# The sign pass of a float64-to-float32 conversion, moved from ScalarE to GpSimd

## The chip, the cores and the metric

One core of one Trainium2 chip. The metric is the device time of a run in microseconds (us). Every run quoted here is of the fast state, but for the two kernels without attention near the end (micro and micro2): they ran once each, so their state is unknown. Ratios with an interval are computed as the mean time of one kernel's fast runs over the mean time of the other's fast runs in the same rounds, so they are not quite the ratio of the medians that are quoted beside them.

## The reference, cut to what matters

A sketched linear attention is followed by a token-mixing block. What matters here is the mixing: two 1088 x 1088 token weight matrices that arrive as float64 and are needed as float32.

```python
def reference(**kw):
    attn_out = _attn_ref(q, k, v, S1, S2)            # (4, 4, 1088, 32)
    x = attn_out.transpose(0, 2, 1, 3).reshape(4, 1088, 128)
    theta = x @ w_theta
    zr, zi = x * np.cos(theta), x * np.sin(theta)
    y = np.einsum('ts,bsd->btd', w_tok_r, zr) + np.einsum('ts,bsd->btd', w_tok_i, zi)
    u = x + y
    return u + np.maximum(u @ w_ch, 0.0)
```

## The kernel before

The weights come as 34 pieces of 128 x 544 float64 values, seen as pairs of 32-bit words. For each piece three ScalarE passes and two VectorE instructions build the float32 bits: the scaled high word is shifted left by 3, and a "step" is added whose low 16 bits come from the low word and whose high 16 bits (a float16 with the bits that restore the sign) come from the high word.

```python
    def load_f32(dst, src):
        ...
        st = stg.tile([P, PIECE], I64, tag="st", name="st")[:p, :n]        # 4 buffers
        nc.sync.dma_start(st, src)
        lo, hi = split(st)
        step = stg.tile([P, PIECE, 2], I16, tag="step", name="step", bufs=2)[:p, :n]
        x = dst.bitcast(I32)
        A.activation(dst, hi.bitcast(F32), AF.Copy, scale=2.0**-112)                            # L122
        A.activation(step[:, :, 1].bitcast(F16), hi.bitcast(F32), AF.Copy, scale=2.0**-60)      # L123, the sign pass
        A.activation(step[:, :, 0], lo.bitcast(U32), AF.Copy, scale=2.0**-29)                   # L124
        ts(x, x, 3, ALU.logical_shift_left)                                                     # VectorE, L85
        tt(V, x, x, step.rearrange("p n t -> p (n t)").bitcast(I32), ALU.add)                   # VectorE, L81
    # ... cut ...
    for i in range(NK):
        for n in range(0, S, PIECE):
            load_f32(wT[:, i, n:n + PIECE], w_tok[i][:, n:n + PIECE])
    with tc.high_priority(offset=p1 - p0 + 1000):     # batch 0's keys and queries, interleaved with the pieces
        keys([0], first=True)
        for g in range(NG):
            queries(0, g)
```

`A` is ScalarE, `V` and `ts` are VectorE. A scheduler fixes the order of instructions on each engine when the kernel is built.

Of the kernel before, what the change touches and what calls it, by code (L numbers as in the profile page):

```python
# [21 lines left out]
F32 = mybir.dt.float32  # L22
F16 = mybir.dt.float16
# [4 lines left out]
AF = mybir.ActivationFunctionType  # L28
ALU = mybir.AluOpType
# [14 lines left out]
def kernel(  # L44
# [11 lines left out]
    nc = tc.nc  # L56
# [21 lines left out]
    V, A = nc.vector, nc.scalar  # L78

    def tt(eng, o, a, b, op):  # L80
        eng.tensor_tensor(out=o, in0=a, in1=b, op=op)  # L81

    def ts(o, a, s1, op0, s2=None, op1=None):
        kw = {} if op1 is None else {"op1": op1}
        V.tensor_scalar(out=o, in0=a, scalar1=s1, scalar2=s2, op0=op0, **kw)  # L85
# [8 lines left out]
    def split(t):  # L94
        w = t.bitcast(I32).rearrange("p (n t) -> p n t", t=2)
        return w[:, :, 0], w[:, :, 1]
# [9 lines left out]
    def load_f32(dst, src):  # L106






        p, n = dst.shape
        if src.dtype == F32:
            nc.sync.dma_start(dst, src)
            return
        st = stg.tile([P, PIECE], I64, tag="st", name="st")[:p, :n]
        nc.sync.dma_start(st, src)
        lo, hi = split(st)
        step = stg.tile([P, PIECE, 2], I16, tag="step", name="step", bufs=2)[:p, :n]  # L120
        x = dst.bitcast(I32)
        A.activation(dst, hi.bitcast(F32), AF.Copy, scale=2.0**-112)  # L122
        A.activation(step[:, :, 1].bitcast(F16), hi.bitcast(F32), AF.Copy, scale=2.0**-60)  # L123
        A.activation(step[:, :, 0], lo.bitcast(U32), AF.Copy, scale=2.0**-29)  # L124
        ts(x, x, 3, ALU.logical_shift_left)
        tt(V, x, x, step.rearrange("p n t -> p (n t)").bitcast(I32), ALU.add)
# [502 lines left out]


    load_f32(w2.rearrange("p t n -> p (t n)"), w_sq.rearrange("p t n -> p (t n)"))
    A.mul(w2[:, 0], w2[:, 0], 1.0 / (2.0 * math.pi))
    def keys(bs, first=False):
# [10 lines left out]
# [3 lines that stand above are left out]
# [60 lines left out]
```

## Time and profile before

| | before |
|---|---|
| time, median of 4 runs | 401.69 us (400.59 to 402.77) |
| busy in the load stage, 10 to 92 us: ScalarE / VectorE / GpSimd | 74.8 / 69.6 / 0 us |
| batch 0's feature work begins on VectorE | 91.76 us |

The profile has one row for each engine: PE is TensorE's matmuls, PEld its weight loads, DVE VectorE, ACT ScalarE, POOL GpSimd. "Busy" counts instructions that run. An instruction that has been issued but is held up inside the engine counts as busy too. The lines themselves are shown in the prediction.

### The profile page before, as it was taken

To read this page: it belongs to the slowest core of one execution; us is meant where nothing else is said; L and a number is where in the kernel's file an instruction comes from. 1 tells how busy PE (TensorE), PEld (TensorE's weight loads), DVE (VectorE), ACT (ScalarE), POOL (GpSimd) and SP (SyncE) were. 2 spreads that over 40 slices of the span, in tenths; PEclk is the share of its full clock that TensorE was granted. 3 is DMA by queue.
4 is the path that set the end of the run, shared out by engine and by line. 5 is a ranking of instruction groups with operands and counts; after the bars stand their busy time and mean duration, and the time that the engine had idled before them with its cause. 6 is when DMAs were issued, how large, how long until landed. Compare 5 with 4: busy or idle time off the path is not lost.

```text
span 400.2 us, 4502 instructions
## 1 busy us (share of the span) xinstructions
PE 292.0 (73%) x1633; PEld 212.7 (53%) x1633; DVE 241.2 (60%) x618; ACT 148.3 (37%) x309; POOL 0.7 (0%) x6
## 2 busy tenths in 40 slices
PE   1720741261389999999453489999889999899995
PEld 0610540140367876878232366756567666667663
DVE  5788978888924457467676822376923459543111
ACT  3779999993043332210022022313032431132100
POOL 0000000000000000000000000000000000000000
PEclk9975575556569999999756558999959999989999
DMA  7677888830000121110000000120000100001100
GB/s 271 227 259 250 300 248 286 299 140 2 0 0 2 52 69 59 59 61 2 1 0 0 2 0 0 41 75 0 2 0 0 58 0 2 0 0 41 36 21 16
DMA packets 11606, 28.82 MB, mean 72 GB/s; under 512 B 1216, under 2 KB 5568, under 8 KB 11584
## 3 DMA queue, kind: packets, MB, share of 16 engines
q1 hardware_dynamic: 11584, 28.53, 21.5%
q8 instruction: 13, 0.21, 0.2%
q14 instruction: 9, 0.07, 0.1%
HBM read 26.30 MB, written 2.23 MB: 71 GB/s over the span
## 4 chain that ended last, share of the span: by engine, by line
PE 56%; DVE 20%; ACT 15%; DMA 6%; issue 1%; SPq 1%; DVEq 0%; ACTq 0%
PE y L604 28%; PE w L557 4%; DMA st<-w_tok 4%; ACT step L123 4%; ACT step L124 4%; PE w L577 3%; PE acc L341 3%; PE acc L436 3%; PE w L426 3%; DVE lv L81 3%; ACT wT L122 2%; DVE qp L81 2%; PE w L551 2%; PE w L618 2%; PE w L572 2%; DVE fl L88 2%
## 5 line engine op out<-in xcount | busy, mean ns | idle before, releaser
L604 PE MATMUL y<-wT,zst 128*128 128x384 f32 (+1 forms) x384 | 135.3, 485 | 0.4 <-DVE zst L81 0.4
L604 PEld LDWEIGHTS y<-wT,zst 128*128 128x128 f32 x384 | 69.1, 195 | 29.3 <-issue 1.3
L341 PE MATMUL acc<-ksl 128*128 128x128 f16 (+1 forms) x216 | 23.8, 273 | 17.8 <-DVE ksl L88 17.8
L555 ACT COPY qpT<-w 128x256 f32<-128x256 f32 x36 | 13.1, 369 | 51.7 <-PE w L551 51.5
L557 PEld LDWEIGHTS w<-kvbd,qpT 128*128 128x128 f32 x144 | 24.5, 239 | 13.7 <-ACT qpT L555 11.8
L341 PEld LDWEIGHTS <-ksl 128*128 128x128 f16 x216 | 18.2, 110 | 22.2 <-DVE ksl L88 11.5
L557 PE MATMUL w<-kvbd,qpT 128*128 128x64 f32 x144 | 26.7, 328 | 4.1 <-ACT qpT L555 3.8
L81 DVE CUSTOM_DVE_ANT_0 wT<-wT,step 128x1088 uint16<-128x1088 uint16 x34 | 24.3, 719 | 8.0 <-ACT step L124 7.8
L123 ACT ACTIVATE step<-st 128x544 f16<-128x544 f32 (+1 forms) x35 | 27.8, 794 | 0.0
L124 ACT ACTIVATE step<-st 128x544 int16<-128x544 uint32 (+1 forms) x35 | 27.3, 781 | 0.0
L574 ACT COPY xT<-w 128x384 f32<-128x384 f32 x12 | 5.8, 479 | 56.1 <-PE w L572 56.1
L85 DVE TENSOR_SCALAR tn<-w 128x384 f32<-128x384 f32 x12 | 6.7, 558 | 32.8 <-PE w L577 32.8
L551 PE MATMUL w<-ident,qp 128*128 128x128 f32 x72 | 15.8, 336 | 14.6 <-DVE qp L81 14.6
L122 ACT ACTIVATE wT<-st 128x544 f32<-128x544 f32 x34 | 22.9, 679 | 4.8 <-DMA st<-w_tok 4.8
L485 ACT COPY lv<-w 128x288 f32<-128x288 f32 x36 | 13.2, 401 | 22.0 <-PE w L484 21.9
L625 ACT ACTIVATE ot<-w 128x384 f32<-128x384 f32 (+2 forms) x16 | 6.1, 406 | 39.2 <-PE w L618 29.9
L551 PEld LDWEIGHTS w<-ident,qp 128*128 128x128 f32 x72 | 11.3, 190 | 15.9 <-issue 15.8
L81 DVE TENSOR_TENSOR ot<-ot,w 128x384 f32<-128x384 f32 (+2 forms) x16 | 6.9, 449 | 18.6 <-ACT ot L625 18.6
L436 PEld LDWEIGHTS acc<-ld_v,kp 128*128 128x128 f32 x144 | 17.0, 192 | 0.7
L436 PE MATMUL acc<-ld_v,kp 128*128 128x64 f32 x144 | 17.4, 274 | 0.0
L81 DVE TENSOR_TENSOR uT<-xT,y 128x384 f32<-128x384 f32 (+1 forms) x12 | 6.3, 527 | 17.0 <-PE y L604 17.0
L577 PEld LDWEIGHTS w<-w,xT 128*128 128x128 f32 x72 | 12.3, 247 | 7.0 <-ACT xT L574 6.4
(217 smaller groups left out, 502.2 us busy)
## 6 DMA issues: line engine op xcount, KB each, us to landing
st<-w_tok SPq DMA_DIRECT2D x34, 544.0 KB, 4.8
ld_k<-k_l SPq DMA_DIRECT2D x4, 576.0 KB, 3.9
ld_q<-q_l SPq DMA_DIRECT2D x4, 576.0 KB, 4.9
ld_v<-v_l SPq DMA_DIRECT2D x4, 576.0 KB, 6.0
out<-ot SPq DMA_DIRECT2D x8, 192.0 KB, 2.1
out<-ot SPq DMA_DIRECT2D x4, 128.0 KB, 1.8
st<-w_sq SPq DMA_DIRECT2D x1, 256.0 KB, 3.8
out<-ot SPq DMA_DIRECT2D x4, 32.0 KB, 1.8
```

The costliest lines, as they stand in the source:

```text
L81: eng.tensor_tensor(out=o, in0=a, in1=b, op=op)
L122: A.activation(dst, hi.bitcast(F32), AF.Copy, scale=2.0**-112)
L123: A.activation(step[:, :, 1].bitcast(F16), hi.bitcast(F32), AF.Copy, scale=2.0**-60)
L124: A.activation(step[:, :, 0], lo.bitcast(U32), AF.Copy, scale=2.0**-29)
L341: nc.tensor.matmul(gp[:, r0 * P:(r0 + s1 - s0) * P], ks[:, a, cs], ks[:, s0:s1, cs], skip_group_check=True, **kw)
L436: nc.tensor.matmul(kv[:, n], kp[:, i * H + 2 * n:i * H + 2 * n + 2].rearrange("p h i j -> p (h i j)"), vn[:, c, 2 * n:2 * n + 2].rearrange ...
L485: A.copy(lv[:, :, :, c].rearrange("p l t n -> p (l t) n"), lp.rearrange("p (x n) -> p x n", n=HR))
L551: nc.tensor.transpose(tr[:, n * P:(n + 1) * P], qp[:, i * H + 2 * n:i * H + 2 * n + 2].rearrange("p h i j -> p (h i j)"), ident)
L555: A.copy(qpT.rearrange("p n t -> p (n t)"), tr[:, :2 * P])
L557: nc.tensor.matmul(num[:, i * P + n * 2 * D:i * P + (n + 1) * 2 * D], qpT[:, n], kvbd[b][:, n], start=True, stop=True)
L577: nc.tensor.matmul(th[:, i * P:(i + 1) * P], xT[:, i * P:(i + 1) * P], w2[:, 0], start=True, stop=True)
L604: nc.tensor.matmul(yp[:, :t1 - t0], z, wT[:, i, t0:t1], start=(i == 0), stop=(i == NK - 1))
```

## The change

The intent is to take one of three passes from the engine that sets the pace and give it to an engine that does nothing.

```diff
         A.activation(dst, hi.bitcast(F32), AF.Copy, scale=2.0**-112)
-        A.activation(step[:, :, 1].bitcast(F16), hi.bitcast(F32), AF.Copy, scale=2.0**-60)
+        nc.gpsimd.tensor_scalar(out=step[:, :, 1].bitcast(F16), in0=hi.bitcast(F32), scalar1=2.0**-60,
+                                scalar2=None, op0=ALU.mult)
         A.activation(step[:, :, 0], lo.bitcast(U32), AF.Copy, scale=2.0**-29)
```

With the change the line numbers in the file are one higher from here on: ScalarE's third pass becomes L125.

## The prediction

> **What bounds the kernel now.** I read the busy shares by slice first, then the stretches, the waits, and last the chain of work that ended last. In the page of the kernel before, each slice is 10 us:
>
> ```profile
> PE   1720741261389999999453489999889999899995
> DVE  5788978888924457467676822376923459543111
> ACT  3779999993043332210022022313032431132100
> DMA  7677888830000121110000000120000100001100
> ```
>
> There are two parts. Up to about 92 us the token weights are loaded and converted (34 pieces of 128x544 float64), while batch 0's key and query work runs between the pieces. From about 111 us TensorE is nearly always busy. Between them lie 20 us of VectorE work alone. The change touches the first part only. Its stretches (columns: PE, PEld, DVE, ACT, POOL busy, granted clock, DMA share, GB/s):
>
> ```profile
> 10.00:92.00 82.00, 32.60 (x209) 25.52 (x209) 69.55 (x242) 74.76 (x129) 0.00 (x0) 0.65 0.73 245
> 60.00:70.00 10.00, 1.01 (x7) 0.48 (x7) 8.90 (x32) 10.00 (x17) 0.00 (x0) 0.50 0.83 285
> 92.00:112.00 20.00, 6.13 (x25) 4.55 (x26) 18.90 (x33) 2.37 (x6) 0.00 (x0) 0.52 0.01 1
> ```
>
> ScalarE is the fullest engine, 74.8 of 82 us, and has no gap at all from 60 to 70 us; VectorE is close behind with 69.6 us. So ScalarE sets the pace, but VectorE has only 12.5 us to spare. The groups of a piece, as they are in that stretch or on the page:
>
> ```profile
> L123 ACT ACTIVATE step<-st 128x544 f16<-128x544 f32 (+1 forms) x35 | 27.8, 794 | 0.0
> L124 ACT ACTIVATE step<-st 128x544 int16<-128x544 uint32 (+1 forms) x35 | 27.3, 781 | 0.0
> L122 ACT ACTIVATE wT<-st 128x544 f32<-128x544 f32 x34 | 22.9, 679 | 4.8 <-DMA st<-w_tok 4.8
> L81 DVE CUSTOM_DVE_ANT_0 wT<-wT,step 128x1088 uint16<-128x1088 uint16 x34 | 24.3, 719 | 8.0 <-ACT step L124 7.8
> L85 DVE TENSOR_SCALAR wT<-wT 128x544 int32<-128x544 int32 x34 | 14.4, 432 | 0.1
> ```
>
> VectorE's add waits for ScalarE's second step pass for 7.8 us in all; ScalarE in turn waits 4.8 us for the load. The chain shows where this reaches the end. Here are three consecutive pieces on it, and the point at which the conversion lets go (start, us, what):
>
> ```profile
> 66.34 0.71 ACT step L123
> 67.05 0.65 ACT step L124
> 67.70 0.54 ACT wT L122
> ...
> 90.30 0.72 ACT step L124
> 91.04 0.72 DVE wT L81
> 91.76 0.98 DVE fl L88
> ```
>
> One piece advances in 0.71 + 0.65 + 0.54 = 1.90 us. Batch 0's feature work on VectorE (the line fl) stands behind the last converted piece in VectorE's fixed order, and everything after follows from it. So a shift of this moment should move the end by nearly as much.
>
> **What the Trainium skill says.** First, "SBUF — State Buffer", section Who interferes with whom: GpSimd's only SBUF read and write ports are VectorE's second pair. A VectorE instruction in a 2-port mode contends for it, and one with two SBUF inputs contends with a GpSimd instruction that reads SBUF; whichever starts first holds the pair for its whole duration. The trace before has no GpSimd work beside VectorE, so it neither confirms nor denies this. Second, "VectorE: DVE Perf Modes", section The perf-mode tier table: a float32 tensor_scalar between SBUF tensors runs at 2x with both ports. The trace fits: the 544-element shift takes 0.432 us, while the 576-element two-input product on the same engine takes 0.75 us. So the shift, the add (two inputs), and most of the feature work are all contending instructions. Third, "GPSIMD Engine Reference", section Performance versus the Vector engine: a tight one-input loop took 1.8 cycles an element at 1.2 GHz, 769 ns for 512 elements. An estimate from it for 544 elements is 0.82 us. The only comparable instruction in the trace is a 128x128 select of 0.29 us on GpSimd; estimated by elements alone this would be 1.23 us for 544, an upper figure, as part of it is fixed. I take 0.8 us, with 0.6 to 1.2 as its doubt.
>
> **The change part by part.** Removed: 34 full passes on ScalarE (and one short one for the square weights). By their pitch in the chain, 0.65 to 0.71 us each, that is 34 x 0.68 = 23 us. ScalarE's busy time in the stretch falls from 74.8 to about 52 us: it can no longer set the pace. Per piece it needs 0.54 + 0.65 = 1.2 us.
>
> Added: 34 GpSimd passes of an estimated 0.8 us, 27 us in all, on an engine that is empty here. Alone this would be hidden: two step buffers let GpSimd work up to two pieces ahead of VectorE's add.
>
> Moved: the instruction order of the changed kernel shows GpSimd doing only these passes after its setup. VectorE has the same work in nearly the same order; batch 0's query slices come three pieces before the last add, where before they were cut among the last five. A load's buffer is now freed when both ScalarE and GpSimd have read it.
>
> So the next limits are these. The load: 299 GB/s at a DMA share of 0.86 in the best slice makes an estimated 345 GB/s at full share; 245 GB/s x 82 us = 20.1 MB would need 58 us. It isn't the bound. VectorE: 69.6 us busy, plus about 5 us of idle that doesn't come from ScalarE (12.5 less 7.8), is 75 us. That is the floor if nothing contends, 7 us below the 82.
>
> With contention, GpSimd's 27 us have to be fitted beside VectorE. Reductions and operations that read PSUM are free of it; from the rows for this stretch they make some 5 us of the 69.6. That leaves about 64 us of contending VectorE work. If the pair is held exclusively, the two engines together need 64 + 27 = 91 us, and the free 5 us can lie beside GpSimd; some waits of VectorE on TensorE remain. I get 92 to 97 us for the stretch, 10 to 15 us more than now. If GpSimd manages to hide half of its time in VectorE's start-up gaps between small instructions, it is 75 + 13.6 = 88.6 us, 6.6 us more. I choose a value between, **+10 us**: 401.6 + 10 = 411.6, or **412 us**. Later parts have no GpSimd work, and their lengths should stay.
>
> **The rivals.** First, *ScalarE relieved, little contention*. For it: ScalarE plainly sets the pace from 56 to 70 us, GpSimd is empty, and it can run ahead. Against it: almost every VectorE instruction in the stretch has the form that the page says collides. It would give the 75 us floor, 7 us less, 394 to 395 us; without the last ScalarE passes cutting into batch 0's feature copies perhaps another us. Even this is only just at 2%.
>
> Second, *exclusive port*, my choice, 408 to 417 us: VectorE becomes the bound with GpSimd's time added to it.
>
> Third, *GpSimd itself slow*: input elements lie 8 bytes apart and 16-bit results 4 bytes apart, and nothing in the trace shows what GpSimd does with that. At 1.2 us and an exclusive port the stretch is 64 + 41 = 105 us or more, 425 us; at 1.9 us a piece GpSimd alone would pace the stage as ScalarE does now.
>
> Fourth, *the load takes over*: buffers are released in a different order, and the four of them must cover a landing time of 4.8 us. At four buffers and a pitch near 2 us there are 8 us for landing and reading, so this should only matter where GpSimd falls behind. It would leave the time about as it is.
>
> **Range and chances.** The gain has a floor set by VectorE's own 69.6 us, about 7 us; the loss has a long tail with GpSimd's unknown duration. I take 397 to 425 us for eight in ten. Faster by over 2% (below 393.5) needs no contention and a little more besides: 0.12. Within 2% (to 409.6) covers weak or half hidden contention: 0.35. Slower: 0.53.
>
> **What would show each step.** Right: ScalarE's busy time in the stage near 52 us with many gaps; the shift and the add, and the 1152-element feature operations, longer than 0.43, 0.72 and 1.35 us while GpSimd runs and unchanged after it has finished; the last add at 100 to 105 us instead of 91; the same length from there to the end. Wrong: VectorE's durations unchanged and the last add before 86 us would mean the ports hardly collide; a GpSimd pass much over 1.2 us with idle VectorE waiting for it would mean that the engine, not the port, is slow; ScalarE or GpSimd waiting for loads for over 10 us would mean that the transfers took over; and an end that moves less than the last add would mean that this moment was not on the path.

## The result, and the profile after

The changed kernel takes **414.68 us** (413.43 to 414.83, 4 runs) against 401.69: ratio 1.0317, 95% interval 1.0282 to 1.0351. It is slower by 13 us. The result is still correct.

The busy tenths of the kernel after, in 40 slices of 10.3 us:

```profile
PE   1721262026238999999745459999979899899995
DVE  5899979996992454665875942455942358734111
ACT  3567547663204424130013122323023332042100
POOL 2768889965000000000000000000000000000000
```

ScalarE has gaps everywhere in the first ten slices; VectorE is now the full one. GpSimd is busy for most of the stage. The stretches of the kernel after (columns: PE, PEld, DVE, ACT, POOL busy, granted clock, DMA share, GB/s):

```profile
10.00:92.00 82.00, 26.45 (x153) 21.17 (x153) 77.15 (x228) 51.17 (x82) 66.79 (x33) 0.80 0.77 245
104.00:124.00 20.00, 5.65 (x22) 4.13 (x23) 19.36 (x35) 2.93 (x7) 0.00 (x0) 0.57 0.00 1
```

ScalarE went from 74.8 to 51.2 us in the same 82 us; part of its work now lies behind 92 us, and up to the feature work it went from 74.5 to 56.1 us (two fences of that stretch stand below). VectorE went from 69.6 to 77.2 us in the same stretch although it got through fewer instructions (228, before 242). The 20 us of VectorE work that followed the stage at 92 us now follow it at 104 us. The groups that belong to a piece:

```profile
L123 POOL TENSOR_SCALAR step<-st 128x544 f16<-128x544 f32 (+1 forms) x35 | 73.4, 2097 | 25.2 <-DMA st<-w_sq 7.3
L125 ACT ACTIVATE step<-st 128x544 int16<-128x544 uint32 (+1 forms) x35 | 27.8, 803 | 11.3 <-DVE wT L81 11.3
L122 ACT ACTIVATE wT<-st 128x544 f32<-128x544 f32 x34 | 23.3, 686 | 11.4 <-DMA st<-w_tok 11.3
L81 DVE CUSTOM_DVE_ANT_0 wT<-wT,step 128x1088 uint16<-128x1088 uint16 x34 | 24.9, 732 | 4.6 <-POOL step L123 4.0
L85 DVE TENSOR_SCALAR wT<-wT 128x544 int32<-128x544 int32 x34 | 18.3, 543 | 0.0
```

A pass takes 0.794 us on ScalarE and 2.097 us on GpSimd. The wait has turned round: VectorE's add waited 7.8 us for ScalarE before; now ScalarE waits 11.3 us for VectorE's add, and VectorE waits only 4.0 us for GpSimd. The shift has grown from 432 to 543 ns; the add hardly (719 to 732). On the chain of the kernel after (start, us, what), VectorE stands where ScalarE stood:

```profile
95.92 0.76 DVE wT L81
96.67 1.28 DVE q L88
...
103.47 0.32 PE acc L199 x2
103.82 0.17 DVE pw L205
104.25 0.98 DVE fl L88
```

What is left out between them are TensorE's query slices and a matmul that stands behind them. So here the last converted piece no longer releases the feature work: the last add runs from 99.95 to 100.68 us, and VectorE then waits 3.0 us for that matmul. What both kernels have in common is VectorE's last product on the queries (the line q): in all nine kernels of the table below the feature work begins 6.6 to 7.7 us after this product starts, while the last add starts anywhere from 0.6 us (before) to 12.0 us (step3) ahead of it.

The feature work (fl) begins at 104.25 us, before at 91.76: 12.5 us later. From there to the end of the profiled span it is 411.7 - 104.25 = 307.5 us, before 400.2 - 91.76 = 308.4. So the whole loss lies ahead of that moment.

What holds VectorE up is best seen at its smallest instructions. Two of them before, in VectorE's timeline (start, us, what):

```profile
71.78 0.16 DVE L88 SCALAR_TENSOR_TENSOR own<-ipn,hm 128x4 f32<-128x4 f32 x1
...
72.63 0.22 DVE L85 TENSOR_SCALAR gm<-gm,sab 128x4 f32<-128x4 f32 x1
```

The same two after, with a neighbour, and the GpSimd pass that ran meanwhile, from 83.92 to 85.68 us:

```profile
84.09 0.52 DVE L88 SCALAR_TENSOR_TENSOR own<-ipn,hm 128x4 f32<-128x4 f32 x1
...
85.01 0.69 DVE L85 TENSOR_SCALAR gm<-gm,sab 128x4 f32<-128x4 f32 x1
85.14 0.57 DVE L85 TENSOR_SCALAR nz<-nl 128x8 f16<-128x8 f32 x1
```

```profile
83.92 1.76 POOL L123 TENSOR_SCALAR step<-st 128x544 f16<-128x544 f32 x1 [0.30 <-DVE wT L81]
...
94.43 5.48 POOL L123 TENSOR_SCALAR step<-st 128x544 f16<-128x544 f32 x1 [2.86 <-DVE wT L81]
```

Four-element instructions of 0.16 and 0.22 us take 0.52 and 0.69 us, and the second and third come free together, at 85.70 us, when the pass ends. The second GpSimd line shows the reverse. From 94.4 to 98.3 us VectorE runs long instructions without a gap, and a pass that needs 1.8 us takes 5.48 us.

Up to the feature work, both kernels run some 243 VectorE instructions:

```profile
10.00:91.76 81.76, 32.60 (x209) 25.52 (x209) 69.31 (x242) 74.52 (x128) 0.00 (x0) 0.65 0.73 246
```

```profile
10.00:104.25 94.25, 33.79 (x209) 26.64 (x209) 84.70 (x244) 56.12 (x93) 72.27 (x34) 0.76 0.67 213
```

The first is before, the second after. VectorE's busy time grows by 84.70 - 69.31 = 15.4 us, its idle time shrinks from 12.5 to 9.6 us, and 15.4 - 2.9 = 12.5 us is the delay.

### The profile page after: what moved, and what is told of

The parts are those of the page before. It is cut to its first block, busy times and chain, and to the rows that moved or that the text cites. A ratio compares the mean times of both kernels' runs of the same rounds, so it can differ in the third digit from the quotient of the medians.

```text
span 411.7 us, 4555 instructions
## 1 busy us (share of the span) xinstructions
PE 291.4 (71%) x1633; PEld 212.3 (52%) x1633; DVE 256.6 (62%) x618; ACT 130.1 (32%) x274; POOL 74.1 (18%) x41
## 4 chain that ended last, share of the span: by engine, by line
PE 56%; DVE 29%; ACT 4%; issue 4%; POOL 2%; DMA 2%; SPq 1%; DVEq 0%; ACTq 0%; POOLq 0%
PE y L605 28%; PE w L558 4%; PE acc L437 4%; PE w L578 3%; DVE wT L81 3%; PE acc L342 3%; DVE lv L81 2%; PE w L427 2%; DVE wT L85 2%; POOL step L123 2%; DVE qp L81 2%; PE w L573 2%; PE w L619 2%; PE w L552 2%; DVE fl L88 2%
## 5 line engine op out<-in xcount | busy, mean ns | idle before, releaser
L123 POOL TENSOR_SCALAR step<-st 128x544 f16<-128x544 f32 (+1 forms) x35 | 73.4, 2097 | 25.2 <-DMA st<-w_sq 7.3
L342 PE MATMUL acc<-ksl 128*128 128x128 f16 (+1 forms) x216 | 22.6, 264 | 19.6 <-DVE ksl L88 19.6
L125 ACT ACTIVATE step<-st 128x544 int16<-128x544 uint32 (+1 forms) x35 | 27.8, 803 | 11.3 <-DVE wT L81 11.3
L122 ACT ACTIVATE wT<-st 128x544 f32<-128x544 f32 x34 | 23.3, 686 | 11.4 <-DMA st<-w_tok 11.3
L552 PE MATMUL w<-ident,qp 128*128 128x128 f32 x72 | 15.4, 330 | 14.0 <-DVE qp L81 14.0
L437 PE MATMUL acc<-ld_v,kp 128*128 128x64 f32 x144 | 18.8, 287 | 3.3 <-DVE kp L81 3.3
L437 PEld LDWEIGHTS acc<-ld_v,kp 128*128 128x128 f32 x144 | 18.2, 203 | 4.2 <-DVE kp L81 3.5
L85 DVE TENSOR_SCALAR wT<-wT 128x544 int32<-128x544 int32 x34 | 18.3, 543 | 0.0
```

The source lines that it names most:

```text
L85: V.tensor_scalar(out=o, in0=a, scalar1=s1, scalar2=s2, op0=op0, **kw)
L123: nc.gpsimd.tensor_scalar(out=step[:, :, 1].bitcast(F16), in0=hi.bitcast(F32), scalar1=2.0**-60, scalar2=None, op0=ALU.mult)
L342: nc.tensor.matmul(gp[:, r0 * P:(r0 + s1 - s0) * P], ks[:, a, cs], ks[:, s0:s1, cs], skip_group_check=True, **kw)
L437: nc.tensor.matmul(kv[:, n], kp[:, i * H + 2 * n:i * H + 2 * n + 2].rearrange("p h i j -> p (h i j)"), vn[:, c, 2 * n:2 * n + 2].rearrange ...
L552: nc.tensor.transpose(tr[:, n * P:(n + 1) * P], qp[:, i * H + 2 * n:i * H + 2 * n + 2].rearrange("p h i j -> p (h i j)"), ident)
```

## The experiments

My theory after the result: **hold-up**. GpSimd's passes hold VectorE up at a shared port, and VectorE's lengthened work is the delay. (That the place is a port is what the prediction cites for it; the runs show which instructions are held up, and for how long.) The rivals: **slow engine** (a GpSimd pass is late, and VectorE waits for its result), **buffers** (GpSimd keeps the load or step buffers too long) and **order** (the scheduler placed the work differently). In what follows "the relief" is ScalarE's freedom from the sign pass. "Features" is the moment at which fl begins, and "VectorE" its busy time from 10 us to that moment, both in the profiled run. pool_free is slower than before, but its interval lies on both sides of 2%, so by that mark alone its verdict is "unclear".

| run | time, us | before, same rounds | ratio (95%) | features | VectorE |
|---|---|---|---|---|---|
| before | | | | 91.76 | 69.3 |
| after | 414.68 | 401.69 | 1.032 (1.028 to 1.035) | 104.25 | 84.7 |
| no_sign | 397.83 | 400.35 | 0.993 (0.986 to 1.000) | 87.97 | 68.9 |
| pool_tiny | 398.04 | 401.87 | 0.990 (0.985 to 0.994) | 88.13 | 69.4 |
| pool_half | 402.41 | 402.82 | 1.002 (0.997 to 1.007) | 94.28 | 76.4 |
| pool_side | 414.18 | 400.35 | 1.032 (1.026 to 1.038) | 103.98 | 86.9 |
| pool_free | 410.48 | 401.87 | 1.020 (1.014 to 1.025) | 101.02 | 84.7 |
| before_side | 413.64 | 400.35 | 1.031 (1.025 to 1.036) | 102.95 | 86.7 |
| step3 | 414.65 | 401.87 | 1.031 (1.027 to 1.035) | 105.57 | 86.4 |

### The relief alone

```diff
-        step = stg.tile([P, PIECE, 2], I16, tag="step", ...)          # zeroed once, two tiles in turn
+        step = stepz[nst[0] % 2][:p, :n]; nst[0] += 1
-        A.activation(step[:, :, 1].bitcast(F16), ...)                  # no sign pass at all
```

> The sign pass is left out altogether, the sign half of the step tiles being zero once and for all (wrong on purpose). If ScalarE's load was the pace and the loss of the change comes from GpSimd, this shows the gain that the relief alone is worth: VectorE's floor, 392 to 396 us. If the loss came from the changed instruction order, it stays above 405 us.

397.83 us, 0.7% below before, a little above the range. The scheduler has placed the work for a relieved ScalarE here, and there is no loss, so such an order is not enough to cause one. But the relief is worth only some 2.5 us: features begin 3.8 us earlier. The stretch shows why:

```profile
10.00:87.97 77.97, 31.92 (x209) 24.98 (x209) 68.88 (x243) 54.94 (x94) 0.00 (x0) 0.80 0.75 257
```

VectorE's idle time fell only from 12.5 to 9.1 us. I had taken 5 us as what ScalarE does not cause. With ScalarE nearly gone as a cause (2.4 us of waits for its conversion passes are left), other waits grew: one alone, for a TensorE result of batch 0's chain, is 4.1 us. It comes after the last add, which starts at 82.6 us, 8.4 us earlier than before. So the conversion itself gained more than the prediction's 7 us, and in this order of instructions the queries' chain kept over half of it. Whether another order would keep more was not tested.

### GpSimd's passes without anyone waiting for them

```diff
+        junk = stg.tile([P, PIECE, 2], I16, tag="junk", name="junk", bufs=1)[:p, :n]
+        nc.gpsimd.tensor_scalar(out=junk[:, :, 1].bitcast(F16), in0=hi.bitcast(F32), ...)
```

added to no_sign (pool_side), or to the kernel before with its ScalarE pass kept (before_side). In pool_free the pass reads a constant tile instead of the loaded piece.

> As no_sign, but GpSimd makes the same pass from the same loaded piece into a tile that nobody reads (wrong on purpose). VectorE never waits for GpSimd here; only the load buffers do. Port theory: nearly all of the loss remains, 409 to 416 us. Slow-engine theory (VectorE waits for a late GpSimd result): the loss goes, 393 to 399 us.

> The kernel before, its ScalarE pass kept, with GpSimd's pass added beside it into a tile that nobody reads (right result). Port theory: VectorE's busy time in the load stage grows by about 15 us, of which its idle 12.5 us takes only a part: 407 to 415 us. Slow-engine theory: only the load buffers feel it, 401 to 404 us.

> As pool_side, but GpSimd's passes read a constant tile, so nothing waits for them and they wait for nothing: not even the load buffers can carry a delay (wrong on purpose). They run back to back from about 8 us, some 34 x 1.9 = 65 us. Port theory: most of the loss is still there, 407 to 415 us. If the loss in pool_side came through load buffers that GpSimd kept, 396 to 401 us.

All three fell in the ranges of the hold-up theory. In pool_side nobody reads what GpSimd writes, and the time is that of the changed kernel. The stretch:

```profile
10.00:103.98 93.98, 32.71 (x209) 25.65 (x209) 86.90 (x244) 54.74 (x93) 69.19 (x34) 0.78 0.64 213
```

Against no_sign, VectorE is busy 86.90 - 68.88 = 18.0 us longer with the same work, and features begin 16.0 us later. So a late result is not what costs. Nor is the order: no_sign, pool_tiny, pool_half, pool_side and pool_free have the same sequence of VectorE operations and tiles up to the features, and so have before and before_side. Paired one by one, the growth lies in instructions that are shorter than 0.3 us in no_sign (15 us) and in the shift (4.4 us); the add gives 1.3 us back. Nor is it the load buffers: in pool_free nothing depends on GpSimd in any way, and most of the loss is still there. It is smaller than in pool_side; the passes ran back to back from 2.2 to 74.0 us, so that the last part of the stage had none beside it. before_side has the cost without the relief, and loses 3.1% too.

### A third step tile

```diff
-        step = stg.tile([P, PIECE, 2], I16, tag="step", name="step", bufs=2)
+        step = stg.tile([P, PIECE, 2], I16, tag="step", name="step", bufs=3)
```

> The changed kernel with three step tiles instead of two (right result). In its trace ScalarE waited 11.3 us and GpSimd 6.2 us for VectorE's add, that is for a free step tile. Port theory: VectorE is the bound and those waits are only its echo, 412 to 416 us. If the missing buffer was a cause, 405 to 411 us.

414.65 us, as expected: ScalarE's wait for VectorE's add fell from 11.3 to 6.4 us, and nothing came of it. The wait was an echo of the busy VectorE, as far as this run can tell: its order of instructions changed too.

### The dose

```diff
-        nc.gpsimd.tensor_scalar(out=step[:, :, 1].bitcast(F16), in0=hi.bitcast(F32), ...)
+        nc.gpsimd.tensor_scalar(out=step[:, :n // 2, 1].bitcast(F16), in0=hi[:, :n // 2].bitcast(F32), ...)   # pool_half; pool_tiny: 32 columns
```

Both use the zeroed step tiles of no_sign.

> The changed kernel with GpSimd doing only the first half of each piece's sign pass, the other half staying zero (wrong on purpose). By itself such a pass took 1.04 us, the full one 1.80 us. Port theory: the loss goes with the time for which GpSimd holds the port, so about half of the way from no_sign (397.8) to pool_side (414.2): 404 to 408 us. Theory of a fixed cost for each pass (start-up, a lock taken once for a fixed time): 411 to 414 us.

> As pool_half, with 32 of the 544 elements in a pass. If the loss goes with the time for which GpSimd works, a pass of an estimated 0.3 us costs next to nothing: 397 to 400 us. If there is a fixed cost for each pass, it shows here: over 400 us.

pool_tiny is no_sign, within noise: 34 GpSimd instructions as such cost nothing, though each was on record for 0.63 us on average. pool_half came out at 402.41, below its range of 404 to 408: a missed size. Its VectorE time lies 7.5 us over no_sign's, or 0.22 us a pass, while the full pass in pool_side costs 18.0 us, or 0.53 us a pass. So the hold-up grows a little faster than a pass's length (1.04 and 1.80 us, next section). The direction is that of the theory, and the 8-element form below shows the same ratio; what makes it so stays open.

### The disputed costs by themselves

Two kernels without attention run GpSimd passes and VectorE instructions alone and side by side. Each part starts when the one before has ended.

```python
segment(p_kernel, 4)                    # GpSimd alone; also half the elements, dense input, dense output, ...
segment(None, 0, v_shift, 24)           # VectorE alone
segment(p_kernel, 4, v_shift, 24)       # both together
```

> No attention kernel: the sign pass on GpSimd by itself in several forms, then eight kinds of VectorE instruction alone and again beside four sign passes. The output is zeros, wrong on purpose. Port theory (VectorE is held up while GpSimd has the shared port): beside GpSimd, the 2-port forms (shift, float16 result of 1152, 8-element scale) and the two-input forms (add, products) take longer in total by about 0.45 us per GpSimd pass, as the changed kernel's VectorE busy time grew by 15 us over 34 passes; the reduction and the PSUM-reading form do not. If the port were held for a whole pass it would be about 1.8 us per pass. Slow-engine theory (the pass itself is slow): a pass alone takes 1.7 to 1.8 us, not the 0.8 us that I estimated, and denser input or output or half the elements shortens it; then VectorE totals change little.

GpSimd without VectorE's test instructions beside it (only set-up copies and memsets of VectorE ran meanwhile), in its timeline (start, us for the whole group), four passes each: the kernel's form on 272 elements, and a dense float32 one on 1088:

```profile
24.91 4.14 POOL L110 TENSOR_SCALAR pstep<-st 128x272 f16<-128x272 f32 x4
...
38.56 12.10 POOL L110 TENSOR_SCALAR pf<-dense 128x1088 f32<-128x1088 f32 x4
```

Three passes of the kernel's form take 5.41 us, or 1.80 us each; a dense float32 pass of 544 takes 1.63 us and one of 1088 takes 3.03 us. So an element costs (3.03 - 1.63) / 544 = 2.6 ns, and about 0.2 us is fixed. Reading every other word costs nothing (1.65 us), writing every other 16-bit word 0.15 us (1.78 us). VectorE's shift alone, and beside four passes:

```profile
105.35 8.53 DVE L121 TENSOR_SCALAR vi<-sgn 128x544 int32<-128x544 int32 x24
...
117.91 12.70 DVE L121 TENSOR_SCALAR vi<-sgn 128x544 int32<-128x544 int32 x24
```

| VectorE form | alone | beside 4 passes | per pass |
|---|---|---|---|
| shift, 544 int32 (one input) x24 | 8.53 us | 12.70 us | 1.0 us |
| scale to float16, 1152 (one input) x14 | 9.44 | 13.61 | 1.0 |
| scale, 8 elements (one input) x80 | 5.95 | 9.91 | 1.0 |
| add of the kernel (two inputs) x14 | 8.97 | 10.82 | 0.46 |
| product, 128 (two inputs) x40 | 8.16 | 10.01 | 0.46 |
| product, 1152 (two inputs) x8 | 10.23 | 11.62 | 0.35 |
| maximum over 1152 (reduction) x8 | 10.16 | 10.16 | 0 |
| scale of a PSUM tile, 512 x14 | 8.45 | 8.45 | 0 |

The forms that the port should touch are held up, the other two not at all. One-input forms lose twice as much, and not the whole 1.8 us of a pass. The small set-up copies on GpSimd at the start of each part are in these numbers, so "per pass" is a little high. Why not the whole pass is seen in single shifts. Three in a row, and the pass that ran beside them:

```profile
118.61 0.90 DVE L121 TENSOR_SCALAR vi<-sgn 128x544 int32<-128x544 int32 x1
119.43 0.43 DVE L121 TENSOR_SCALAR vi<-sgn 128x544 int32<-128x544 int32 x1
119.78 1.02 DVE L121 TENSOR_SCALAR vi<-sgn 128x544 int32<-128x544 int32 x1
...
118.47 2.04 POOL L110 TENSOR_SCALAR pstep<-st 128x544 f16<-128x544 f32 x1
```

One pass holds VectorE up twice, early and late, by about 0.5 and 0.6 us over the shift's 0.43, and between the two a shift runs at its usual length. The other three passes show the same.

> No attention kernel, zeros out on purpose: four VectorE forms alone and beside GpSimd passes of 272, 544 and 1088 elements and beside GpSimd memsets, which read nothing. If the hold-up goes with the length of a pass, the shift (2-port) loses about 0.5, 1.0 and 2.0 us per pass and the product of 128 elements 0.23, 0.46 and 0.9. If the page is right that a two-input form collides only with a GpSimd instruction that reads, the product and the add lose nothing beside memsets, and the shift still does.

For the lengths this missed (for the memsets it held), and it taught the most. VectorE's 40 shifts alone, beside eight passes of 272, and beside six memsets on GpSimd:

```profile
20.85 14.17 DVE L121 TENSOR_SCALAR vi<-sgn 128x544 int32<-128x544 int32 x40
...
39.19 14.17 DVE L121 TENSOR_SCALAR vi<-sgn 128x544 int32<-128x544 int32 x40
...
110.75 19.78 DVE L121 TENSOR_SCALAR vi<-sgn 128x544 int32<-128x544 int32 x40
```

And the first of the eight passes on GpSimd:

```profile
39.35 14.84 POOL L110 TENSOR_SCALAR pstep<-st 128x272 f16<-128x272 f32 x1
```

Here VectorE lost nothing, and a 1.04 us pass took 14.84 us: it ended only 0.8 us after the last shift had. It was the same with five passes of 544 beside the shifts (VectorE 14.17 us), the products (12.20 us alone and beside), and the adds (15.33 and 15.32), though the same pass had held the same forms up in the first kernel. Beside three passes of 1088 VectorE lost again, 5.7 us with the shifts, 0.9 us with the products and 2.7 us with the adds. So either side can win in a stream of equal instructions. The 8-element scale lost every time: 150 of them took 11.09 us alone, 14.57 beside eight passes of 272, 16.01 beside five of 544 and 16.76 beside three of 1088, which is 0.43, 0.98 and 1.89 us a pass. The first two stand in the ratio 0.44, close to the 0.22 / 0.53 = 0.42 of pool_half and pool_side. That fits a kernel whose losses are mostly those of small instructions, as the pairing above shows. Memsets, which read nothing, hold up the shift by 5.6 us over 5.7 us of memsets, and the product (12.20) and the add (15.33) not at all.

### Other places for the pass

> The sign pass on VectorE itself instead of GpSimd (right result), estimated at the shift's pitch of 0.36 us: 34 of them are 12.2 us of VectorE time, a little less than the 15 us that GpSimd's passes cost VectorE in the changed kernel. If VectorE's time sets the stage once ScalarE is relieved, 405 to 411 us: no better than before although nothing waits for GpSimd. If ScalarE's relief were worth more than no_sign showed, 396 to 402 us.

> ScalarE keeps two thirds of the sign passes, VectorE takes every third (right result). ScalarE loses about 11 x 0.68 = 7.5 us, VectorE gains about 11 x 0.36 = 4 us of its idle 12.5. If both engines bound the stage in turn, as the runs so far say, this is near the best split: 397 to 401 us. If VectorE's idle time can't be used, 402 to 405 us.

> ScalarE keeps four fifths of the sign passes, GpSimd takes every fifth (right result). ScalarE loses 7 x 0.68 = 4.8 us; VectorE is held up by 7 x 0.45 = 3 us. Port theory: relief and hold-up nearly cancel, 398 to 403 us, far below the 414.7 us of the full change; if any use of GpSimd in the stage cost the whole loss, over 410 us.

```diff
-        nc.gpsimd.tensor_scalar(out=step[:, :, 1].bitcast(F16), in0=hi.bitcast(F32), scalar1=2.0**-60, ...)
+        ts(step[:, :, 1].bitcast(F16), hi.bitcast(F32), 2.0**-60, ALU.mult)     # sign_dve: all on VectorE
```

In the mixes a counter sends every third pass to VectorE, or every fifth to GpSimd; ScalarE keeps the others. All three came out level with before: sign_dve 402.23 us (ratio 1.000, 0.996 to 1.005), mix_dve3 402.22 (0.999, 0.996 to 1.002), mix_pool5 402.25 (0.999, 0.995 to 1.003). mix_pool5 is as expected: one fifth of the passes on GpSimd gives back about what it relieves. mix_dve3 lies at the edge of the second of its two ranges, while before was higher in these rounds too (402.82); by the ratio the split neither gains nor loses. sign_dve missed: I expected 405 to 411 us. Its VectorE passes took 16.1 us of busy time, yet its ratio to before is 1.000, against 1.032 with the pass on GpSimd. Its schedule isn't comparable, since features begin at 88.14 us but a part of batch 1's key work and one add were placed after them; so I don't read its 402 us as a measure of VectorE's time. No version with a right result beats the kernel before by more than noise. no_sign, which leaves the pass out, and pool_tiny say that 0.7 to 1.0% is about all there is in the order that the scheduler makes.

## Why the prediction was right

I gave 412 us, 397 to 425, with 0.53 on slower; it is 414.68. The mechanism was right, two of its terms were wrong in opposite directions, and so the closeness of 412 to 414.68 is in part luck.

- **ScalarE relieved**: "from 74.8 to about 52 us", measured 51.2 in the same 82 us. Right in kind; the number is helped by the longer stage. Up to the feature work the fall is 18.4 us (74.5 to 56.1), not 23.
- **The path**: "a shift of this moment should move the end by nearly as much". Features shifted by 12.5 us, the profiled spans by 11.5, the medians by 13.0. Right. But that features stand "behind the last converted piece" holds only for the kernel before. The last add moved by 8.9 us (91.04 to 99.95, at the early edge of the 100 to 105 us that I named), and the features by more, because they wait for the query slices. VectorE's lengthened work ahead of the last query product is what moved them.
- **VectorE becomes the bound, held up by GpSimd**: right, and shown by pool_side, before_side and pool_free, in which the hold-up stands alone.
- **The length of a pass**: "I take 0.8 us, with 0.6 to 1.2 as its doubt". Measured: 1.80 us alone, 2.1 us in the kernel. Wrong by more than a factor of two; the page gives the figure as the best case of a tight loop, and I took it as the middle. The upper figure from the select, 1.23 us, was nearer and still short.
- **The port held for a whole pass**: "If the pair is held exclusively, the two engines together need 64 + 27 = 91 us". With the true pass length that sum would be 64 + 61 = 125 us, and the stretch was 94 us. VectorE ran many instructions while one pass was under way. It was held up by 15.4 us over 34 passes, 0.45 us each, a quarter of a pass. The two errors nearly cancelled: 27 us of passes, of which I let 10 count, against 61 to 72 us of passes, of which 12.5 counted.
- **Which instructions would be longer**: the shift, yes (432 to 543 ns); the add and the 1152-element operations hardly (the add 719 to 732). The time went into the shift and the many small instructions.
- **The rival of relief without contention**: its 7 us gain was an overestimate for the time; no_sign has 8.4 us at the last add, but 3.8 us at the features and 0.7% in the time, because the queries' chain comes in between.
- **The rival of a slow engine**: half true. The engine is slow, but VectorE's wait for it is 4.0 us, and pool_side without any wait is no faster.
- **The rival of the load**: its sign, "ScalarE or GpSimd waiting for loads for over 10 us", came true (ScalarE waits 11.3 us) and misled: in no_sign ScalarE waits 11.5 us for loads and nothing is lost, and in pool_side it waits 3.8 us and all is lost. As far as these runs show, a relieved ScalarE only arrives early.
- **Two slips on which nothing rests**: 299 / 0.86 is 348 GB/s, not 345; and the first three lines of the chain are three steps of one converted piece, not three converted pieces.

What stays open: what decides which engine wins at the port, why a pass holds VectorE up in two stretches and not in proportion to its length, whether another order would keep more of the relief, and how sign_dve's time divides.

## What to carry to other kernels

An idle engine is not a free one if it shares a port with the next-busiest engine: before moving work, look at what the engine that will be the bound afterwards loses, not at what the present bound gains. Measure the moved instruction by itself, and test the relief alone by leaving the work out; here that showed a ceiling of about 1%, in this order of instructions, before any cost. And when busy time of an engine grows for the same instructions, look at its smallest ones: a four-element operation that takes 0.69 instead of 0.22 us is waiting inside.

## What the Trainium skill lacked or had wrong

- "GPSIMD Engine Reference", section Performance versus the Vector engine: it has 1.8 cycles an element as the best case of a tight loop, 769 ns for 512 elements, and no figure for a tensor_scalar. The tensor_scalar here cost 2.6 ns an element, which at the page's 1.2 GHz is 3.1 cycles, plus about 0.2 us: 1.63 us for 544 dense float32 elements. Its section Engine selection calls one-input operations "roughly line-rate"; VectorE's shift of as many elements takes 0.432 us.
- "SBUF — State Buffer", section Who interferes with whom: it says that whoever issues first gets the shared pair for the whole instruction. For the GpSimd side the runs show otherwise: 24 shifts beside four passes of 1.8 us lost 1.0 us a pass, not 1.8, and a shift ran at its usual 0.43 us in the middle of a pass. What it doesn't say is that VectorE can keep the pair from one instruction to the next: beside 40 shifts in a row a pass of 1.04 us took 14.84 us.
- The same section was right on which forms collide: the reduction (10.16 us) and the PSUM-reading form (8.45 us) lost nothing, and beside memsets the shift lost (14.17 to 19.78 us) while the two-input product did not (12.20 us). It does not give the sizes: about 1.0 us a pass for one-input forms in a 2-port mode and 0.35 to 0.46 us for two-input forms where GpSimd wins.
- No page that I read gives the cost of a 16-bit output at every other place on GpSimd: 1.78 against 1.63 us for 544 elements.
